# Layer norm scaling moved to VectorE with a lookahead of two pairs, four exp buffers, and an up-projection split in halves

## The chip, the cores and the metric

The kernel runs on one core of a Trainium2 chip. The metric is device time in microseconds (us) of one execution. A core has five engines that run at the same time, each through its own instructions in order: TensorE (PE, matrix products, whose weight loads are listed apart as PEld), VectorE (DVE), ScalarE (ACT), GpSimd (POOL) and SyncE (SP, here only for DMA). An instruction that waits on a semaphore holds back all that stands behind it on its engine.

## The reference

```python
xn  = layernorm(x)                               # x: 2048 tokens x 448, no gain or bias
q, k, v = split(xn @ wqkv)                       # 16 heads of 28
pq, pk  = q @ w_phi[h], k @ w_phi[h]             # 28x28 per head
phi_q = concat(softmax(pq), softmax(-pq))        # 56 features per head
phi_k = concat(softmax(pk), softmax(-pk))
kv, z = phi_k.T @ v, sum(phi_k, over tokens)     # needs every token
o     = (phi_q @ kv) / (phi_q @ z + 1e-6)
h     = xn @ w1 + b1                             # 448 -> 1792
out   = x + o @ wo + mish(h) @ w2
```

## The kernel before, in words

The 2048 tokens are 16 tiles of 128; a pair is two tiles, so there are 8 pairs. Everything stays in SBUF.

**Start.** Loads go out on the queues of SP, ACT and POOL. The 28x28 matrices of `w_phi` are laid as blocks on the diagonal of `Wbd`, which POOL has set to zero; four small DMAs on POOL's queue do it (lines 234 to 236). `w_trans` and `w_mm` fold `Wbd` into the key and query weights once (`Wp`), so that pk and pq come straight from xn.

**Pair loop (lines 472 to 494).** For pair j: `ln` takes statistics on DVE (`bn_stats`, `bn_aggr`), 1/sqrt(var + eps) on POOL (`ln_rstd`, lines 257 and 259), and the scaling `xn = (x - mean) * rstd` (`ln_norm`, line 263) on DVE for pairs 0 and 1 and on POOL for pairs 2 to 7. `xT` transposes xn on PE, and ACT copies it to `xnT`. `vproj` and `kproj` are 8 matmuls each; DVE copies v out of PSUM (line 314), and `kexp` takes exp(pk) and exp(-pk) on ACT into one of two buffers `Ek` (line 330). `knorm` sums each head on DVE (line 335), takes the reciprocal (line 337), and POOL multiplies (line 338), which makes `phi_k`; it runs one pair behind. `qproj` and `qexp` do half of a 512-token group of pq per pair, and give exp(pq), exp(-pq) as `EqT`. `masks` on POOL (lines 240 to 246) stands in pair 2.

**Up-projection loop (lines 499 to 507).** 28 steps n, each with 8 matmuls of the up-projection (`ffn1`, line 420: two halves of 512 tokens, in two PSUM banks) and one Mish on ACT (line 430). After step 5 stands `kvz` (128 matmuls, line 365): kv and z for all heads, masked by DVE into `KVZ`. From step 6 on each step also does `nd` of one tile: 4 matmuls for each sign (line 384) into banks 6 (sign 0) and 7 (sign 1), which hold numerator and denominator, and five DVE operations (lines 390 to 398) and one on POOL that divide them. The two signs are unnormalised exps, so line 391 forms the ratio of the two softmax sums. Three steps later `oTr` transposes the result (line 406).

**Down-projection (lines 433 to 451).** For each tile 14 matmuls with `w2` and 4 with `wo` into one bank; DVE adds x, and SP stores.

**Order.** The program is written out engine by engine in the order of the Python calls. The class `Prog` adds the semaphore waits by itself from the names that each operation reads (`r`), writes (`w`) and the PSUM banks that it uses (`x`). A buffer's name in `w` makes the operation wait for the last readers; a bank in `x` makes it wait for the other engines' last use of that bank.

Of the kernel before, what the change touches and what calls it, by code (L numbers as in the profile page):

```python
# [12 lines left out]
D = 448  # L13
# [144 lines left out]
def _kernel(es, nc, x2, A_wqkv, A_w_phi, A_wo, B_w1, B_b1, B_w2, out2):  # L158
# [38 lines left out]
    hm = [sb(f"hm{i}", [P, FC, 1024]) for i in range(2)]  # L197
    hm0 = hm[0].rearrange("p a b -> p (a b)")
    EK0 = 7 * 1024
    Ek = [hm0[:, EK0 + i * 4 * D:EK0 + (i + 1) * 4 * D].rearrange("p (t s f) -> p t s f", t=2, s=2) for i in range(2)]  # L200
    WT = hm0[0:KP, 0:2 * KC * D].rearrange("p (w c n) -> p w c n", w=2, c=KC)
    phik = hm[1].rearrange("p a b -> p (a b)").rearrange("p (t f) -> p t f", t=NT)
    rq = [sb(f"rq{i}", [P, 2, H], FP32) for i in range(2)]
# [139 lines left out]

    def qproj(tc, gp):
        for u in range(2):
# [67 lines left out]
    def ffn1(n):  # L413
        tcp, fc = n // FC, n % FC
        b = 2 * (n % 2)
        def f(e):
            for u in range(2):
                for c in range(KC):
                    o = tcp * 1024 + u * 512
                    i = e.matmul(PS[:, b + u, :], W1[:, c, fc * P:(fc + 1) * P], xnT[:, c, o:o + 512],  # L420
                                 start=(c == 0), stop=(c == KC - 1))
# [117 lines left out]
```

## Time and profile before

| | |
|---|---|
| three runs | 208.52, 210.96, 212.55 us (median 210.96) |
| the profiled execution | 212.34 us, of which the span of the trace is 210.4 us |
| PE busy | 181.3 us (86% of the span) |
| ACT busy | 84.5 us (40%) |
| DVE busy | 83.3 us (40%) |
| POOL busy | 76.6 us (36%) |
| TensorE clock granted, mean | 0.959 of full speed |

How to read it: the shares are means over stages that differ. The chain of work that ended last is 65% PE, 17% POOL, 9% ACT, 4% DVE and 3% DMA. The span falls into the start and the pair loop (to about 84 us), the up-projection loop (84 to 153 us) and the down-projection (153 us to the end). In rows of matmuls a group's duration reaches from the start of its first to the modelled end of its last; the next group can start before that end.

### The profile page before, as it was taken

How to read it: one execution, taken by the hardware profiler on the slowest of the kernel's cores; microseconds unless marked ns; L12 is line 12 of the kernel's file. 1: busy time of each engine (PE TensorE's matmuls, PEld its weight loads, DVE VectorE, ACT ScalarE, POOL GpSimd, SP SyncE). 2: the span in 40 equal slices, each digit the busy share in tenths (PEclk: the TensorE clock that was granted, in tenths of full speed). 3: DMA queues.
4: the chain of work that ended last, by engine and by line, in shares of the span. 5: the costliest groups of instructions: out<-in, count | busy, mean ns of one | idle time of the engine just before them, and what ended most of it. 6: DMA issues, size and time to landing. Idle time of an engine off the chain costs nothing.

```text
span 210.4 us, 2756 instructions
## 1 busy us (share of the span) xinstructions
PE 181.3 (86%) x1153; PEld 98.0 (47%) x1153; DVE 83.3 (40%) x160; ACT 84.5 (40%) x94; POOL 76.6 (36%) x70
## 2 busy tenths in 40 slices
PE   0587689395894896899999999999999999999994
PEld 0545355142452443349645555554455555555551
DVE  1524085471961564001377777773011212112121
ACT  2536562808438573962246666667720000000000
POOL 8366449999996329200033333442000000000000
PEclk9999699887899797999999999999999999999999
DMA  6999800000000000000000000000001011010101
GB/s 164 281 311 274 241 2 0 0 0 5 2 0 0 0 0 0 3 2 0 3 0 0 3 0 0 3 0 0 3 0 44 29 40 44 22 44 22 47 22 44
DMA packets 7180, 8.69 MB, mean 41 GB/s; under 512 B 576, under 2 KB 6464, under 8 KB 7168
## 3 DMA queue, kind: packets, MB, share of 16 engines
q1 hardware_dynamic: 6544, 8.09, 13.5%
q10 hardware_dynamic: 464, 0.40, 0.6%
q8 instruction: 9, 0.15, 0.3%
q0 software_dynamic: 160, 0.03, 0.1%
q14 instruction: 3, 0.02, 0.0%
HBM read 6.68 MB, written 1.84 MB: 40 GB/s over the span
## 4 chain that ended last, share of the span: by engine, by line
PE 65%; POOL 17%; ACT 9%; DVE 4%; DMA 3%; issue 1%; ACTq 0%; POOLq 0%; DVEq 0%
PE PS L439 20%; PE PS L420 19%; POOL xn L263 7%; POOL hm L338 6%; PE PS L444 6%; PE PS L310 4%; PE PS L384 4%; ACT hm L330 3%; PE PS L365 3%; PE PS L323 3%; DMA Wbd<-in_A_w_phi_dram 3%; ACT EqT L356 2%; PE PS L406 2%; PE PS L349 2%; POOL rstd L259 1%; PE PS L284 1%
## 5 line engine op out<-in xcount | busy, mean ns | idle before, releaser
L420 PE MATMUL PS<-xnT,W 112*128 112x512 bf16 x224 | 52.5, 381 | 0.6 <-ACT hm L430 0.6
L439 PE MATMUL PS<-W,hm 128*128 128x448 bf16 x224 | 45.0, 353 | 0.0
L430 ACT ACTIVATE hm<-PS,b1T 128x1024 bf16<-128x1024 f32 x28 | 31.2, 1114 | 28.2 <-PE PS L420 28.1
L420 PEld LDWEIGHTS PS<-xnT,W 112*128 112x128 bf16 x224 | 21.0, 98 | 23.3 <-ACT hm L430 1.4
L449 DVE TENSOR_TENSOR out_sb<-PS,x_all 128x448 bf16<-128x448 f32 x16 | 10.0, 625 | 54.5 <-PE PS L444 54.5
L439 PEld LDWEIGHTS PS<-W,hm 128*128 128x128 bf16 x224 | 21.9, 98 | 20.6
L338 POOL TENSOR_TENSOR hm<-hm,rSk 128x1792 bf16<-128x1792 bf16 x8 | 25.7, 3217 | 9.3 <-DVE rSk L337 9.2
L310 PE MATMUL PS<-Wqkv,xnT 112*128 112x448 bf16 x64 | 19.0, 457 | 11.1 <-ACT xnT L301 11.1
L330 ACT ACTIVATE hm<-PS 128x896 bf16<-128x896 f32 x16 | 13.8, 914 | 26.3 <-POOL hm L338 17.1
L263 POOL TENSOR_SCALAR xn<-x_all,mv,rstd 128x448 bf16<-128x448 bf16 x12 | 22.3, 1867 | 0.6
L314 DVE CAST v_ext<-PS 128x896 bf16<-128x896 f32 x8 | 8.8, 1094 | 32.7 <-PE PS L310 32.7
L399 POOL TENSOR_TENSOR o_sb<-t_0,rden 128x448 bf16<-128x448 f32 x8 | 7.5, 943 | 31.8 <-DVE rden L398 31.8
L349 PE MATMUL PS<-xnT,Wp 112*112 112x512 bf16 x64 | 16.4, 402 | 2.0 <-ACT EqT L356 2.0
L356 ACT ACTIVATE EqT<-PS 112x1024 bf16<-112x1024 f32 x16 | 15.6, 1037 | 3.3 <-PE PS L349 3.3
L310 PEld LDWEIGHTS PS<-Wqkv,xnT 112*128 112x128 bf16 x64 | 7.0, 119 | 20.7 <-ACT xnT L301 13.5
L323 PE MATMUL PS<-Wp,xnT 112*128 112x448 bf16 x64 | 15.9, 399 | 0.6 <-ACT hm L277 0.6
L335 DVE TENSOR_REDUCE Sk<-hm 128x64 f32<-128x1792 bf16 x8 | 16.0, 1995 | 0.0
L444 PE MATMUL PS<-Wo,EqT 112*128 112x448 bf16 x64 | 14.8, 352 | 0.0
L399 POOL TENSOR_TENSOR o_sb<-t_1,rden 128x448 bf16<-128x448 f32 x8 | 7.5, 943 | 12.5 <-DVE rden L398 12.5
L349 PEld LDWEIGHTS PS<-xnT,Wp 112*112 112x112 bf16 x64 | 8.1, 135 | 7.3 <-ACT EqT L356 2.5
L323 PEld LDWEIGHTS PS<-Wp,xnT 112*128 112x128 bf16 x64 | 6.9, 111 | 8.7 <-issue 3.7
L251 DVE BATCH_NORM_STATS2 stats<-x_all 128x6 f32<-128x448 bf16 x16 | 9.2, 614 | 4.3 <-DMA x_all<-in_A_x_dram 4.3
(51 smaller groups left out, 153.8 us busy)
## 6 DMA issues: line engine op xcount, KB each, us to landing
W<-in_B_w_dram SPq DMA_DIRECT2D x2, 1568.0 KB, 18.8
out_dram<-out_sb SPq DMA_DIRECT2D x16, 112.0 KB, 1.7
x_all<-in_A_x_dram SPq DMA_DIRECT2D x1, 896.0 KB, 10.3
Wqkv<-in_A_wqkv_dram SPq DMA_DIRECT2D x2, 392.0 KB, 7.6
x_all<-in_A_x_dram SPq DMA_DIRECT2D x2, 224.0 KB, 4.4
x_all<-in_A_x_dram SPq DMA_DIRECT2D x1, 448.0 KB, 7.6
Wqkv<-in_A_wqkv_dram ACTq DMA_DIRECT2D x1, 392.0 KB, 5.0
Wo<-in_A_wo_dram SPq DMA_DIRECT2D x1, 392.0 KB, 22.0
```

What stands on the lines that cost most here:

```text
L263: eng(lambda v: v.tensor_scalar(xn[t % NXN][:, :], x_all[:, t, :], mv[:, t, 0:1], rstd[:, t:t + 1], op0=ALU.subtract, op1=ALU.mult), r=[f" ...
L310: i = e.matmul(PS[:, 2 + u, 0:D], xnT[:, c, t * P:(t + 1) * P], Wqkv[:, c, 2 * D:3 * D], start=(c == 0), stop=(c == KC - 1))
L323: i = e.matmul(PS[:, 4 + u, 0:D], xnT[:, c, t * P:(t + 1) * P], Wp[:, 1, c, :], start=(c == 0), stop=(c == KC - 1))
L330: act(lambda a, s=s: a.activation(Ek[j % 2][:, :, s, :], PS[:, 4:6, 0:D], ACT.Exp, scale=(1.0 if s == 0 else -1.0)), w=[f"Ek{j % 2}{s}"], ...
L335: dve(lambda v: v.tensor_reduce(Sk[b][:, :], Ek[b][:, :, :, :].rearrange("p t s (h f) -> p (t s h) f", f=DH), AX.X, ALU.add), r=[f"Ek{b}0" ...
L338: pool(lambda g: g.tensor_tensor(phik[:, 2 * j:2 * j + 2, :].rearrange("p t (k f) -> p (t k) f", f=DH), Ek[b][:, :, :, :].rearrange("p t s ...
L349: i = e.matmul(PS[0:KP, 6 + u, :], Wp[:, 0, c, g * KP:(g + 1) * KP], xnT[:, c, tc * 512:(tc + 1) * 512], start=(c == 0), stop=(c == KC - 1))
L356: act(lambda a, s=s: a.activation(EqT[:, s, 2 * gp:2 * gp + 2, tc * 512:(tc + 1) * 512], PS[0:KP, 6:8, :], ACT.Exp, scale=(1.0 if s == 0 e ...
L420: i = e.matmul(PS[:, b + u, :], W1[:, c, fc * P:(fc + 1) * P], xnT[:, c, o:o + 512], start=(c == 0), stop=(c == KC - 1))
L430: act(lambda a: a.activation(hm[tcp][:, fc, :].rearrange("p (u n) -> p u n", u=2), PS[:, b:b + 2, :], ACT.Mish, bias=b1T[:, fc:fc + 1]), r ...
L439: i = e.matmul(PS[:, b, 0:D], hm[t // 8][:, fc, o:o + P], W2[:, fc, :], start=(fc == 0), stop=False)
L444: i = e.matmul(PS[:, b, 0:D], oT[:, c, t * P:(t + 1) * P], Wo[:, c, :], start=False, stop=(c == KC - 1))
```

## The change

Five things change. The layer norm scaling of pairs 2 to 7 moves from POOL to DVE (`ln_b`), and the statistics and the scaling of a pair are now issued two pairs ahead of its projections. The transposes of pair j+1 stand in front of `vproj(j)` and no longer behind `kexp(j)`. There are four `Ek` buffers, and `knorm` runs two pairs behind. The four `Wbd` DMAs go out on ACT's queue. In the up-projection loop the two halves of `ffn1` are issued apart, with the `nd` matmuls of sign 1 between them and those of sign 0 behind; `kvz` and all `nd` come one step later. (`vevac` is the copy of v, which stood inside `vproj`; `nd_mm` is the matmuls of `nd`, `nd` what is left of it.)

```diff
-    Ek = [hm0[:, EK0 + i * 4 * D:EK0 + (i + 1) * 4 * D].rearrange("p (t s f) -> p t s f", t=2, s=2) for i in range(2)]
+    Ek = [hm0[:, EK0 + i * 4 * D:EK0 + (i + 1) * 4 * D].rearrange("p (t s f) -> p t s f", t=2, s=2) for i in range(4)]
...
-        dma("POOL", Wbd[DH * j:DH * (j + 1), :, DH * j:DH * (j + 1)],
+        dma("ACT", Wbd[DH * j:DH * (j + 1), :, DH * j:DH * (j + 1)],
...
+    def ln_a(j):
+        for t in (2 * j, 2 * j + 1):
+            ln_stats(t)
+        for t in (2 * j, 2 * j + 1):
+            ln_aggr(t)
+        ln_rstd(2 * j, 2)
+
+    def ln_b(j):
+        for t in (2 * j, 2 * j + 1):
+            ln_norm(t, dve)
...
-    ln(0, dve)
+    ln_a(0)
     w_trans(1, 0)
     w_trans(1, 1)
+    ln_b(0)
     xT(0)
+    ln_a(1)
     w_mm(1, 0)
     w_mm(1, 1)
-    ln(1, dve)
-    ln(2, pool)
+    ln_b(1)
     for j in range(NP):
+        if j + 2 < NP:
+            ln_a(j + 2)
+        if j + 1 < NP:
+            xT(j + 1)
         vproj(j)
+        vevac(j)
+        if j + 2 < NP:
+            ln_b(j + 2)
         if j == 0:
             w_trans(0, 0)
             w_trans(0, 1)
         kproj(j)
         kexp(j)
-        if j + 1 < NP:
-            xT(j + 1)
         if j == 0:
             w_mm(0, 0)
             w_mm(0, 1)
         if j >= 1:
             qproj((j - 1) // 2, (j - 1) % 2)
             qexp((j - 1) // 2, (j - 1) % 2)
-        if j + 3 < NP:
-            ln(j + 3, pool)
+        if j >= 2:
+            knorm(j - 2)
         if j == 2:
             masks()
...
-        if j >= 1:
-            knorm(j - 1)
     qproj(3, 1)
     qexp(3, 1)
+    knorm(NP - 2)
     knorm(NP - 1)
-    KV_AT = 5
+    KV_AT = 6
     for n in range(2 * FC):
-        ffn1(n)
+        m = n - KV_AT - 1
+        ffn1_mm(n, 0)
+        if 0 <= m < NT:
+            nd_mm(m, 1)
+        ffn1_mm(n, 1)
+        mish(n)
+        if 0 <= m < NT:
+            nd_mm(m, 0)
+            nd(m)
         if n == KV_AT:
             kvz()
-        m = n - KV_AT - 1
-        if 0 <= m < NT:
-            nd(m)
         if 0 <= m - 3 < NT:
             oTr(m - 3)
```

On POOL, in the pair loop from the first product for `phi_k` (`hm<-hm,rSk`) on; `xn` is the scaling, `rstd` the two operations of `ln_rstd`. Before:

```order
L338 TENSOR_TENSOR hm<-hm,rSk 128x1792
L257 TENSOR_SCALAR rstd<-mv 128x2
L259 TENSOR_TENSOR rstd<-rstd,mhalf 128x2
L263 TENSOR_SCALAR xn<-x_all,mv,rstd 128x448 x2
L240 MEMSET mask 112x116
L242 AFFINE_SELECT mask<-mask 112x116 x2
L245 MEMSET v_ext 128x256
L246 CAST KVZ<-mask 112x32
L338 TENSOR_TENSOR hm<-hm,rSk 128x1792
```

With the change:

```order
L336 TENSOR_TENSOR hm<-hm,rSk 128x1792
L240 MEMSET mask 112x116
L242 AFFINE_SELECT mask<-mask 112x116 x2
L245 MEMSET v_ext 128x256
L246 CAST KVZ<-mask 112x32
L257 TENSOR_SCALAR rstd<-mv 128x2
L259 TENSOR_TENSOR rstd<-rstd,mhalf 128x2
L336 TENSOR_TENSOR hm<-hm,rSk 128x1792
```

The scaling is gone from POOL. The masks now stand between the first product and the `rstd` of pair 5; each later `rstd` still stands behind a product of an earlier pair.

On DVE, one turn of the pair loop (pair 4); `v_ext` is the copy of v, `Sk` and `rSk` belong to `knorm`. Before, and then with the change:

```order
L314 CAST v_ext<-PS 128x32x28
L251 BN_STATS stats<-x_all 128x6 x2
L254 BN_AGGR mv<-stats 128x2 x2
L335 TENSOR_REDUCE Sk<-hm 128x64
L337 RECIPROCAL rSk<-Sk 128x64
```

```order
L251 BN_STATS stats<-x_all 128x6 x2
L254 BN_AGGR mv<-stats 128x2 x2
L467 CAST v_ext<-PS 128x32x28
L263 TENSOR_SCALAR xn<-x_all,mv,rstd 128x448 x2
L333 TENSOR_REDUCE Sk<-hm 128x64
L335 RECIPROCAL rSk<-Sk 128x64
```

The statistics come ahead of the copy of v, and the scaling stands between that copy and the sums.

On PE, the start of the up-projection loop, through the first two steps with `nd` (`PS<-KVZ,EqT`); `PS<-xnT,W` is the up-projection and `PS<-v_ext,hm` is `kvz`. Before, and then with the change:

```order
L420 MATMUL PS<-xnT,W 128x512 x48
L365 MATMUL PS<-v_ext,hm 112x116 x128
L420 MATMUL PS<-xnT,W 128x512 x8
L384 MATMUL PS<-KVZ,EqT 128x120 x8
L420 MATMUL PS<-xnT,W 128x512 x8
```

```order
L418 MATMUL PS<-xnT,W 128x512 x56
L363 MATMUL PS<-v_ext,hm 112x116 x128
L418 MATMUL PS<-xnT,W 128x512 x4
L381 MATMUL PS<-KVZ,EqT 128x120 x4
L418 MATMUL PS<-xnT,W 128x512 x4
L381 MATMUL PS<-KVZ,EqT 128x120 x4
```

One step of the up-projection more stands ahead of `kvz`, and each later step is cut into halves of four matmuls with four of `nd` behind each.

## Rows read from the trace of the kernel before

**Rows 1.** Windows: stretch, its length, busy by engine (instructions), TensorE clock, DMA share, GB/s.

```profile
31.00:66.00 35.00, 24.99 (x129) 12.91 (x129) 18.87 (x27) 17.86 (x21) 34.20 (x24) 0.90 0.00 1
81.00:84.00 3.00, 3.00 (x9) 1.32 (x8) 0.42 (x1) 0.21 (x1) 3.00 (x2) 0.52 0.00 0
```

**Rows 2.** Who waited for whom: us in total, times, longest us.

```profile
ACT hm L330 <- POOL hm L338: 17.1, 4, 5.5
```

**Rows 3.** Chain of waits, 56 to 66 us: start us, us, what.

```profile
56.39 3.72 POOL xn L263 x2
60.11 3.19 POOL hm L338
...
63.33 1.73 ACT hm L330 x2
65.06 0.92 ACT xnT L301
```

**Rows 4.** Timeline of POOL: start us, us, line, operation, shapes [idle before].

```profile
42.06 0.20 POOL L240 MEMSET mask<- 112x116 f32 x1
...
43.98 3.25 POOL L338 TENSOR_TENSOR hm<-hm,rSk 128x1792 bf16<-128x1792 bf16 x1
47.20 0.24 POOL L257 TENSOR_SCALAR rstd<-mv 128x2 f32<-128x2 f32 x1
47.52 0.72 POOL L259 TENSOR_TENSOR rstd<-rstd,mhalf 128x2 f32<-128x2 f32 x1
```

**Rows 5.** Timeline of DVE in the start and the pair loop.

```profile
6.87 0.70 DVE L263 TENSOR_SCALAR xn<-x_all,mv,rstd 128x448 bf16<-128x448 bf16 x2 [1.18 <-POOL rstd L259]
...
32.74 1.09 DVE L314 CAST v_ext<-PS 128x896 bf16<-128x896 f32 x1 [1.07 <-PE PS L310]
...
45.43 1.99 DVE L335 TENSOR_REDUCE Sk<-hm 128x64 f32<-128x1792 bf16 x1
47.45 0.55 DVE L337 RECIPROCAL rSk<-Sk 128x64 f32<-128x64 f32 x1
```

**Rows 6.** Timeline of PE in the start and the pair loop.

```profile
10.26 0.97 PE L284 MATMUL PS<-Wbd,hm 112*112 112x112 bf16 x8 [1.81 <-DMA Wbd<-in_A_w_phi_dram]
...
22.98 0.94 PE L284 MATMUL PS<-Wbd,hm 112*112 112x112 bf16 x8 [2.67 <-ACT Wp L288]
...
59.49 1.68 PE L323 MATMUL PS<-Wp,xnT 112*128 112x448 bf16 x8
61.01 0.61 PE L298 MATMUL PS<-ident,xn 128*112 128x128 bf16 x8
61.46 1.89 PE L349 MATMUL PS<-xnT,Wp 112*112 112x512 bf16 x8
...
76.66 1.89 PE L349 MATMUL PS<-xnT,Wp 112*112 112x512 bf16 x8
80.58 3.18 PE L349 MATMUL PS<-xnT,Wp 112*112 112x512 bf16 x8 [2.03 <-ACT EqT L356]
```

**Rows 7.** Timeline of PE and DVE in one step of the up-projection loop.

```profile
113.50 0.59 PE L384 MATMUL PS<-KVZ,EqT 112*128 112x120 bf16 x8
...
114.16 1.89 PE L420 MATMUL PS<-xnT,W 112*128 112x512 bf16 x8
114.43 0.17 DVE L391 TENSOR_TENSOR rq<-PS,rq 128x16 f32<-128x16 f32 x1
114.64 0.64 DVE L393 TENSOR_TENSOR t_0<-PS,rq 128x464 f32<-128x464 f32 x1
...
116.01 0.59 PE L384 MATMUL PS<-KVZ,EqT 112*128 112x120 bf16 x8
```

**Rows 8.** Timeline of the DMA issues on POOL's and SP's queues.

```profile
1.82 2.63 POOL L169 DMA_DIRECT2D Wbd<-in_A_w_phi_dram  x4
...
5.22 12.51 SPq L169 DMA_DIRECT2D Wo<-in_A_wo_dram  x1
```

**Rows 9.** DMA issues: queue, count, KB each, median us from issue to landing.

```profile
Wqkv<-in_A_wqkv_dram ACTq DMA_DIRECT2D x1, 392.0 KB, 5.0
```

More of the change, by code (lines that the diff above doesn't have):

```diff
@@ L313, in vproj @@
             pe(f, r=[f"xT{j}", "Wv"], x=[2 + u])
-        dve(lambda v: v.tensor_copy(v_ext[:, 2 * j:2 * j + 2, :, 0:DH],
-                                    PS[:, 2:4, 0:D].rearrange("p t (h d) -> p t h d", d=DH)),
-            w=[f"v{j}"], x=[2, 3])
     def kproj(j):
@@ L329, in kexp @@
         for s in range(2):
-            act(lambda a, s=s: a.activation(Ek[j % 2][:, :, s, :], PS[:, 4:6, 0:D], ACT.Exp,
-                                            scale=(1.0 if s == 0 else -1.0)), w=[f"Ek{j % 2}{s}"], x=[4, 5])
+            act(lambda a, s=s: a.activation(Ek[j % 4][:, :, s, :], PS[:, 4:6, 0:D], ACT.Exp,
+                                            scale=(1.0 if s == 0 else -1.0)), w=[f"Ek{j % 4}{s}"], x=[4, 5])
     def knorm(j):
         b = j % 2
-        dve(lambda v: v.tensor_reduce(Sk[b][:, :], Ek[b][:, :, :, :].rearrange("p t s (h f) -> p (t s h) f", f=DH),
-                                      AX.X, ALU.add), r=[f"Ek{b}0", f"Ek{b}1"], w=[f"Sk{b}"])
+        q = j % 4
+        dve(lambda v: v.tensor_reduce(Sk[b][:, :], Ek[q][:, :, :, :].rearrange("p t s (h f) -> p (t s h) f", f=DH),
+                                      AX.X, ALU.add), r=[f"Ek{q}0", f"Ek{q}1"], w=[f"Sk{b}"])
         dve(lambda v: v.reciprocal(rSk[b][:, :], Sk[b][:, :]), r=[f"Sk{b}"], w=[f"rSk{b}"])
@@ L339, in knorm @@
             phik[:, 2 * j:2 * j + 2, :].rearrange("p t (k f) -> p (t k) f", f=DH),
-            Ek[b][:, :, :, :].rearrange("p t s (h f) -> p (t s h) f", f=DH),
+            Ek[q][:, :, :, :].rearrange("p t s (h f) -> p (t s h) f", f=DH),
             ap_on(rSk[b][:, 0:1], [[1, 4 * H], [0, DH]]), ALU.mult),
-            r=[f"Ek{b}0", f"Ek{b}1", f"rSk{b}"], w=[f"phik{j}"])
+            r=[f"Ek{q}0", f"Ek{q}1", f"rSk{b}"], w=[f"phik{j}"])
     def qproj(tc, gp):
@@ L378, in kvz, with nd_mm, f @@
                     r=["mask"], w=["KVZa0"], x=[6])
-    def nd(t):
-        for s in range(2):
-            def f(e, s=s):
+    def nd_mm(t, s):
+            def f(e):
                 for g in range(QG):
@@ L387, in nd @@
             pe(f, r=[f"Eq{t // 4}{gp}{s}" for gp in range(2)] + [f"KVZa{s}", "KVZ1"], x=[6 + s])
+    def nd(t):
         i = t % 2
@@ L411, in oTr, with ffn1_mm @@
             w=[f"oT{t}"], x=[4])
-    def ffn1(n):
+    def ffn1_mm(n, u):
         tcp, fc = n // FC, n % FC
@@ L416, in f, with mish @@
         def f(e):
[L417 to L421, printed above, removed]
-            return i
-        pe(f, r=["W1"] + [f"xT{j}" for j in range(4 * tcp, 4 * tcp + 4)], x=[b, b + 1])
+            for c in range(KC):
+                o = tcp * 1024 + u * 512
+                i = e.matmul(PS[:, b + u, :], W1[:, c, fc * P:(fc + 1) * P], xnT[:, c, o:o + 512],
+                             start=(c == 0), stop=(c == KC - 1))
+            return i
+        pe(f, r=["W1"] + [f"xT{4 * tcp + 2 * u}", f"xT{4 * tcp + 2 * u + 1}"], x=[b + u])
+    def mish(n):
+        tcp, fc = n // FC, n % FC
+        b = 2 * (n % 2)
         if tcp:
@@ L428, in ffn1 @@
         else:
-            rr = ["Ek00", "Ek01", "Ek10", "Ek11"]
+            rr = [f"Ek{i}{u}" for i in range(4) for u in range(2)]
         act(lambda a: a.activation(hm[tcp][:, fc, :].rearrange("p (u n) -> p u n", u=2), PS[:, b:b + 2, :], ACT.Mish,
@@ L462, in ln, with vevac @@
             ln_norm(t, eng)
-    ln(0, dve)
+    def vevac(j):
+        dve(lambda v: v.tensor_copy(v_ext[:, 2 * j:2 * j + 2, :, 0:DH],
+                                    PS[:, 2:4, 0:D].rearrange("p t (h d) -> p t h d", d=DH)),
+            w=[f"v{j}"], x=[2, 3])
+    def ln_a(j):
[8 more added lines that the diff above has]
+    ln_a(0)
     w_trans(1, 0)
     w_trans(1, 1)
+    ln_b(0)
     xT(0)
+    ln_a(1)
     w_mm(1, 0)
     w_mm(1, 1)
-    ln(1, dve)
-    ln(2, pool)
+    ln_b(1)
     for j in range(NP):
+        if j + 2 < NP:
+            ln_a(j + 2)
+        if j + 1 < NP:
+            xT(j + 1)
         vproj(j)
+        vevac(j)
+        if j + 2 < NP:
+            ln_b(j + 2)
         if j == 0:
```

## The prediction, made before the changed kernel was run

> **What bounds the kernel now.** I read the windows first, then the waits, the chain of waits, and the timelines of POOL, DVE and PE. In the pair loop from 31 to 66 us POOL is busy 34.20 of 35.00 us while PE is busy 24.99 [rows 1]: POOL is the bound there. The chain shows how: scaling of pair 7 (3.72 us) to 60.11, the product for phi_k of pair 3 (3.19), then ACT's two exps, which waited for that product because there are only two `Ek` buffers, then the copy to xnT, and PE goes on at 66.0 [rows 3]. ACT waited 17.1 us in all for POOL in this way [rows 2]. POOL's turn is a product (3.22 from its start to the next operation), two rstd operations (1.04) and the scaling (3.72), some 8.0 us [rows 3, 4]. PE's own work for a pair, from start to start at full clock, is 1.52 for `kproj` and as much for `vproj`, 0.45 for `xT` and 1.73 for half a `qproj` (its 1.89 less 0.16, by which a group's modelled end overlaps the next: 59.49 + 1.68 is 0.16 past 61.01): 5.2 us [rows 6].
>
> A second cost hangs on the idle time. After a wait of 2.03 us the last `qproj` takes 3.18 us where the same eight matmuls took 1.89 [rows 6]; the granted clock in 81 to 84 us is 0.52 [rows 1], so mostly the 1.2 GHz level, and after the wait a stretch runs slow that costs about 1.3 us (3.18 - 1.89).
>
> In the up-projection loop a step lasts 2.51 us (113.50 to 116.01) but PE's work in it is `nd` and `oTr` with 0.66 (113.50 to 114.16) and `ffn1` with 1.89 less the same 0.16, 1.73: 2.39 [rows 7]. So PE waits about 0.1 us per step, and the next `nd` starts only when DVE has let go of banks 6 and 7.
>
> **The pair loop after the change.** The scaling costs 0.70 us per pair on DVE [rows 5] in place of 3.72 on POOL [rows 3]. That row was taken with POOL idle. In the new order POOL is idle beside each scaling too: its next product waits for DVE's reciprocal, which stands behind the scaling. The far bound is POOL's 3.72; I take the row of the same instruction on the same engine.
>
> But POOL and DVE now form a ring, since each `rstd` stands on POOL behind the product of an earlier pair, and the sums on DVE behind the scaling that waits for that `rstd`. One turn: reciprocal done, handover about 0.08 (estimate; handovers in these rows are 0.02 to 0.1), product 3.22, rstd 1.04, handover 0.05, scaling 0.70, sums 2.02, reciprocal 0.55 [rows 4, 5]: 7.66 us. That is hardly under 8.0. The gain therefore does not come from the turn itself, but from when the ring starts, from how few turns there are (pairs 5, 6 and 7), and from what no longer follows the last one.
>
> *Start of the ring.* In the trace of before the copy of v of pair 2 ends at 33.83 (32.74 + 1.09) [rows 5]. What PE does ahead of it changes so: `w_mm(0,1)` at 22.98 waited for ACT [rows 6], where the copy of xT(1), 0.92 [rows 3], no longer stands ahead; xT(3), 0.45, now stands in front of `vproj(2)`. That is about 0.5 earlier, and the short wait for the xnT copy in front of `vproj(2)` is gone. I take 0.8 (between 0 and 1.4), so 33.0. Scaling of pair 4, sums and reciprocal of pair 0: 33.0 + 0.70 + 2.57 = 36.3.
>
> *The ring.* The product of pair 0 runs to 39.6, then the masks, 1.92 (42.06 to 43.98 [rows 4]), which now delay the `rstd` of pair 5, to 41.5; rstd to 42.6, scaling of pair 5 from 42.6. Two turns of 7.66 later, at 57.9, comes the scaling of pair 7, done at 58.6: 1.5 earlier than 60.11.
>
> New waits that this makes: `xT(j+1)` now stands ahead of `vproj(j)` on PE, so a late scaling also holds back `vproj(j)`, `kproj(j)`, and on DVE the copy of v, which stands in front of the next scaling. For pair 5: xT from 43.3, even at the slow clock 0.9, then `vproj(4)` at most 3.2, copy of v to 48.5. The scaling of pair 6 waits for its rstd until 50.2 anyway, so 1.7 us of slack cover it.
>
> *Behind the ring.* PE goes on at 58.65 with xT(7), vproj(6), kproj(6), qproj, vproj(7), kproj(7), and starts the next `qproj` 0.45 + 4 x 1.52 + 1.73 = 8.3 us later at full clock; PE has waited over 2 us by then, so I add one slow stretch of 1.3: 68.3. No exp waits for a buffer: the product of pair 2 ends near 56.8, before `kproj(6)` is done. From that `qproj` to the last one it took 3.92 us (76.66 to 80.58) [rows 6], set by kexp(7) and qexp on ACT, and nothing in that changes. So the last `qproj` starts at 72.2 instead of 80.58: **8.4 us** gained. On POOL the products of pairs 5 to 7 (3 x 3.2) follow the copy of v of pair 7 and the sums of pair 5, near 70.5, and end near 80.5; `kvz` needs them, and seven steps of the up-projection (7 x 1.73) cover that until 87.5. With the old place of `kvz`, one step earlier, 5 us would still be left, so moving it costs and gains nothing.
>
> **The Wbd DMAs.** `w_mm(1,0)` waited 1.81 us for Wbd until 10.26 [rows 6]. On POOL's queue the four issues took 2.63 us [rows 8]. The nearest row on ACT's queue is Wqkv, 5.0 us from issue to landing [rows 9]. Issued behind the memset of Wbd from about 1.5 at POOL's pace, the last lands near 9.1; bounds 8.45 (no wait) and 10.26 (no gain). ACT's issues end near 4.2, and its first copy waits for Wqkv's landing anyway. Whatever is gained here, xT(1), which now stands ahead of `vproj(0)`, takes up (0.9 at the slow clock): I count it in the 0.8 above. The Trainium skill, "DMA: Bandwidth & Descriptors", section "Queues, rings and completion order", says that all DMAs of ACT share one ring on each DMA engine, consumed in order. By that rule Wbd queues behind Wqkv and lands perhaps at 10.3 (estimate), and the total is about 0.5 us worse; no row here shows two DMAs on ACT's queue.
>
> **The up-projection loop.** After the change bank 7 is free after line 393, not after line 396, and bank 6 has half a step more. The new ring: `nd` of sign 1 (0.21), half of `ffn1` (0.87), `nd` of sign 0 (0.21 and 0.16 until its end), lines 391 and 393 (0.21 and 0.64) and about 0.1 of handovers: 2.40 [rows 7], against 2.39 of PE's work. So 2.51 becomes 2.40, 15 intervals: **1.6 us** gained; at best 1.8, at least nothing if a split group starts later. The masked copy `KVZ` (DVE) is now covered by only half a `ffn1`; one time 0.1 at most.
>
> **Sum.** 8.4 + 1.6 = 10.0 us. The profiled execution took 212.34 us (span 210.4), so the same execution would take 202.3 (span 200.4). It lies 1.4 above the median of the runs, 210.96, so I predict **201.0 us**.
>
> **Rivals.**
> - *PE keeps its clock.* If the waits in front of xT(7) and the last `qproj` (about 2.4 and 2.0 us) do not lower it, 2 x 1.3 us fall away: 198.4. For it: the waits are short. Against: one of 2.03 did lower it [rows 6].
> - *The split halves do not pipeline.* Two more changes of group per step; if each shows the 0.16 us by which a group's end overlaps the next [rows 6], the step becomes 2.39 + 0.32 = 2.71 and the loop loses 16 x 0.20 = 3.2 instead of gaining 1.6: 205.8; half of it gives 203.2. Against: the change from `nd` to `oTr` to `ffn1` shows no gap.
> - *The ring is longer.* If the slow clock, or a scaling that takes longer beside other work, uses up the 1.7 us of slack, each microsecond counts twice: 204 to 207.
> - *Slower than before: ACT's queue blocks.* SP's issue of Wo was held for 12.51 us, to 17.7, behind the large loads [rows 8]. If ACT's issues for Wbd were held so long and Wbd landed 5.0 later [rows 9], at 22.7, `w_mm(1,0)` with all of PE behind it would start 12.4 us later than at 10.26 [rows 6]: 213.4, slower than before. It decides from a landing at 20.3 on, 10.0 later than now. Against: ACT's queue has only Wqkv ahead, and SP's hold came at its tenth DMA.
>
> **How the numbers follow.** Forecast 0.65, clock kept 0.13, halves do not pipeline 0.12, longer ring 0.05, ACT blocked 0.05. The forecast's own range is 197.5 to 204.5: start of the ring 0.6 either way, loop 1.6 down to nothing, and 2 us of scatter between runs (208.52 to 212.55). With the clock case below and half of the split case above, the range is 196.0 to 205.5. A measurement of this kernel can tell about 2%, 4.2 us, from no change: faster means below 206.7, slower above 215.2. Nearly all of the first three cases and half of the longer ring lie below 206.7; I take 0.90, 0.07 and 0.03.
>
> **What would show it.** Right: no wait of ACT's exps on POOL; scaling rows on DVE of 0.35 each; scalings of pairs 5, 6 and 7 about 7.7 us apart, each waiting for rstd; the last `qproj` near 72 us; steps of 2.40 us. Wrong: a wait of `w_mm` on Wbd beyond 10.3; steps of 2.5 us or more; scalings of pairs 6 and 7 that wait for the copy of v instead.

## The result, and the profile after

| | before | after |
|---|---|---|
| median of the runs compared | 210.73 us (208.52 to 212.55, 4 runs) | 201.22 us (200.9 to 202.23, 4 runs) |
| profiled execution, span | 212.34, 210.4 us | 200.96, 199.0 us |
| start of the last `qproj` | 80.58 us | 69.27 us |
| interval of an up-projection step | 2.51 us | 2.47 us |
| TensorE clock granted, mean of the span | 0.959 | 0.983 |

The ratio of the two is 0.959, with a 95% interval of 0.9505 to 0.9676: faster. The medians are 9.5 us apart, where 10.0 were forecast. Executions that were slow for their kernel are left out of the ratios (here the one of 212.55), so that a ratio is not the quotient of the medians beside it; this one stands for 8.6 us. The page of the changed kernel, span and busy times by engine:

```profile
span 199.0 us, 2766 instructions
...
PE 176.7 (89%) x1153; PEld 97.9 (49%) x1153; DVE 84.4 (42%) x172; ACT 85.4 (43%) x94; POOL 51.7 (26%) x54
```

POOL lost 24.9 us of work (76.6 to 51.7), most of it the six pairs of scalings at 3.72 [rows 3]; DVE, which took them over at 0.70 a pair, is busy only 1.1 us longer (83.3 to 84.4). That has not made the kernel faster by 24.9 us; the waits say why (engine, line, the releaser, us in all, times, longest us):

```profile
ACT hm L327 <- PE PS L320: 12.0, 8, 3.3
...
DVE xn L263 <- POOL rstd L259: 10.5, 5, 4.0
...
PE PS L298 <- DVE xn L263: 4.8, 3, 2.3
```

ACT's exps (now line 327) wait only for their matmuls, and no more for POOL's product [rows 2]. In its place DVE waits for POOL's `rstd`, and PE for DVE's scaling: the ring that the prediction described. It can be followed on two engines. DVE, scalings of pairs 4 to 7 and one reciprocal (start us, us, line, operation, what ended the idle time before it):

```profile
31.98 0.69 DVE L263 TENSOR_SCALAR xn<-x_all,mv,rstd 128x448 bf16<-128x448 bf16 x2
...
34.64 0.55 DVE L335 RECIPROCAL rSk<-Sk 128x64 f32<-128x64 f32 x1
...
41.50 0.70 DVE L263 TENSOR_SCALAR xn<-x_all,mv,rstd 128x448 bf16<-128x448 bf16 x2 [3.98 <-POOL rstd L259]
...
49.02 0.70 DVE L263 TENSOR_SCALAR xn<-x_all,mv,rstd 128x448 bf16<-128x448 bf16 x2 [2.10 <-POOL rstd L259]
...
56.54 0.70 DVE L263 TENSOR_SCALAR xn<-x_all,mv,rstd 128x448 bf16<-128x448 bf16 x2 [2.10 <-POOL rstd L259]
```

and POOL in the first turn, with the masks in it:

```profile
35.27 3.21 POOL L336 TENSOR_TENSOR hm<-hm,rSk 128x1792 bf16<-128x1792 bf16 x1 [5.43 <-DVE b1T L516]
38.43 0.19 POOL L240 MEMSET mask<- 112x116 f32 x1
...
40.33 0.33 POOL L257 TENSOR_SCALAR rstd<-mv 128x2 f32<-128x2 f32 x1
...
44.80 3.21 POOL L336 TENSOR_TENSOR hm<-hm,rSk 128x1792 bf16<-128x1792 bf16 x1 [3.33 <-DVE rSk L335]
```

The reciprocal of pair 0 ends at 35.19, the product follows, the masks fill 38.43 to 40.3, only then comes `rstd`, and the scaling of pair 5 starts at 41.50. From there on a turn is 7.52 us (41.50, 49.02, 56.54), and the product at 44.80 waits 3.33 us for DVE's reciprocal: the operations of the ring run one after the other on the two engines. Beside POOL's product DVE has, in these turns, only statistics and the copy of v.

PE of the changed kernel, at the places that matter:

```profile
10.23 0.97 PE L284 MATMUL PS<-Wbd,hm 112*112 112x112 bf16 x8 [1.95 <-DMA Wbd<-in_A_w_phi_dram]
...
23.15 0.62 PE L284 MATMUL PS<-Wbd,hm 112*112 112x112 bf16 x8 [2.21 <-ACT Wp L288]
...
41.95 1.01 PE L298 MATMUL PS<-ident,xn 128*112 128x128 bf16 x8 [2.33 <-DVE xn L263]
...
56.99 0.74 PE L298 MATMUL PS<-ident,xn 128*112 128x128 bf16 x8 [2.02 <-DVE xn L263]
...
69.27 3.57 PE L347 MATMUL PS<-xnT,Wp 112*112 112x512 bf16 x8 [2.03 <-ACT EqT L354]
```

The first row answers to that at 10.26 of before [rows 6]: the Wbd DMAs gave nothing. The last answers to 80.58. Beside it the windows (start and end, length, busy time and instructions of PE, PEld, DVE, ACT, POOL, granted clock, DMA share, GB/s):

```profile
41.90:45.00 3.10, 3.04 (x14) 1.72 (x15) 3.06 (x5) 1.02 (x1) 0.20 (x1) 0.53 0.02 5
57.00:60.00 3.00, 3.00 (x21) 1.82 (x22) 2.96 (x4) 1.02 (x1) 0.16 (x1) 1.00 0.00 0
...
69.20:72.70 3.50, 3.44 (x9) 1.67 (x10) 3.31 (x4) 0.01 (x1) 3.50 (x2) 0.53 0.00 0
```

After the waits of 2.33 and 2.03 us PE ran mostly at the 1.2 GHz level (0.53); after the one of 2.02 in front of xT(7) it kept 2.4 GHz (1.00).

Last, one step of the up-projection loop, PE and DVE:

```profile
108.27 0.38 PE L381 MATMUL PS<-KVZ,EqT 112*128 112x120 bf16 x4
...
108.49 1.03 PE L418 MATMUL PS<-xnT,W 112*128 112x512 bf16 x4
...
109.35 0.37 PE L381 MATMUL PS<-KVZ,EqT 112*128 112x120 bf16 x4
...
109.83 0.17 DVE L390 TENSOR_TENSOR rq<-PS,rq 128x16 f32<-128x16 f32 x1 [0.55 <-PE PS L381]
110.04 0.64 DVE L392 TENSOR_TENSOR t_0<-PS,rq 128x464 f32<-128x464 f32 x1
...
110.73 0.22 PEld L381 LDWEIGHTS PS<-KVZ,EqT 112*128 112x128 bf16 x4 [0.42 <-DVE t_0 L392]
110.74 0.38 PE L381 MATMUL PS<-KVZ,EqT 112*128 112x120 bf16 x4
```

`nd` of sign 1 at 110.74 still waits for line 392, 0.42 us of PE's weight loads; DVE's line 390, for its part, starts when sign 0 is done. The ring that was forecast is there, but it is 2.47 us long (108.27 to 110.74).

### The profile page after: what moved, and what is told of

It reads as the page before. It is cut to its first block, busy times and chain, and to the rows that moved or that the text cites. A ratio compares the mean times of both kernels' runs of the same rounds, so it can differ in the third digit from the quotient of the medians.

```text
span 199.0 us, 2766 instructions
## 1 busy us (share of the span) xinstructions
PE 176.7 (89%) x1153; PEld 97.9 (49%) x1153; DVE 84.4 (42%) x172; ACT 85.4 (43%) x94; POOL 51.7 (26%) x54
## 4 chain that ended last, share of the span: by engine, by line
PE 72%; POOL 7%; DVE 7%; ACT 6%; DMA 4%; issue 1%; ACTq 0%; DVEq 0%; POOLq 0%
PE PS L418 21%; PE PS L441 21%; PE PS L446 6%; POOL hm L336 5%; PE PS L310 5%; PE PS L381 4%; DMA Wbd<-in_A_w_phi_dram 4%; PE PS L347 4%; PE PS L363 3%; PE PS L320 3%; DVE Sk L333 3%; ACT EqT L354 2%; PE PS L405 2%; ACT hm L327 2%; PE PS L284 1%; PE PS L298 1%
## 5 line engine op out<-in xcount | busy, mean ns | idle before, releaser
L418 PE MATMUL PS<-xnT,W 112*128 112x512 bf16 x224 | 54.7, 379 | 0.9 <-ACT hm L432 0.9
L418 PEld LDWEIGHTS PS<-xnT,W 112*128 112x128 bf16 x224 | 20.3, 98 | 19.5 <-ACT hm L432 1.4
L310 PE MATMUL PS<-Wqkv,xnT 112*128 112x448 bf16 x64 | 16.3, 407 | 0.0
L320 PE MATMUL PS<-Wp,xnT 112*128 112x448 bf16 x64 | 13.5, 353 | 0.4 <-ACT hm L277 0.4
L381 PEld LDWEIGHTS PS<-KVZ,EqT 112*128 112x128 bf16 x128 | 8.3, 98 | 11.0 <-DVE t_0 L392 3.8
L347 PEld LDWEIGHTS PS<-xnT,Wp 112*112 112x112 bf16 x64 | 8.7, 138 | 8.4 <-ACT EqT L354 2.5
L381 PE MATMUL PS<-KVZ,EqT 112*128 112x120 bf16 x128 | 12.1, 217 | 0.5 <-DVE t_1 L392 0.2
L298 PE MATMUL PS<-ident,xn 128*112 128x128 bf16 x64 | 6.5, 257 | 4.8 <-DVE xn L263 4.8
```

The costliest lines, as they stand in the source:

```text
L320: i = e.matmul(PS[:, 4 + u, 0:D], xnT[:, c, t * P:(t + 1) * P], Wp[:, 1, c, :], start=(c == 0), stop=(c == KC - 1))
L347: i = e.matmul(PS[0:KP, 6 + u, :], Wp[:, 0, c, g * KP:(g + 1) * KP], xnT[:, c, tc * 512:(tc + 1) * 512], start=(c == 0), stop=(c == KC - 1))
```

## The experiments

Each time is a median of device us, and each ratio is against the kernel before, run on the same chip. The edits are on the changed kernel, except the one that is on the kernel before.

### Scaling back on POOL (c5_xn_pool)

```diff
-            ln_norm(t, dve)
+            ln_norm(t, dve if j < 2 else pool)
```

> The changed kernel with the scaling of pairs 2 to 7 back on POOL, lookahead, four Ek buffers and split kept. Theory (turns of POOL and DVE pace the loop): POOL's turn is a product, rstd and scaling, 8.0 us, three turns from the first product near 34 to 35; the scaling of pair 7 ends near 60 to 61 instead of 57.2, 204 us. Rival (the place of the scaling does not matter, the buffers and the lookahead do): 201.2. Rival (the scaling on DVE is nearly all of the gain): 208 or more.

205.29 us (204.48 to 207.12; before 211.05), ratio 0.9752 [0.9695, 0.981]. POOL's scalings of pairs 5 and 7:

```profile
42.05 3.71 POOL L263 TENSOR_SCALAR xn<-x_all,mv,rstd 128x448 bf16<-128x448 bf16 x2
...
58.04 3.71 POOL L263 TENSOR_SCALAR xn<-x_all,mv,rstd 128x448 bf16<-128x448 bf16 x2
```

They are two turns of 8.0 us apart, POOL's own turn of before [rows 4], and the last `qproj` starts at 73.77, 4.5 later. So the move itself is worth about 4 us: each turn is hardly shorter, as predicted, but the last scaling ends at 57.2 and not 61.8. Of these 4.5, 3.0 are the length of that last scaling (3.71 against 0.70), 0.95 the two turns, and 0.55 a later start (42.05 against 41.50). All else in the change, without the move, still gives 5.8 us.

### Two exp buffers (c4_two_ek)

```diff
-    Ek = [... for i in range(4)]
+    Ek = [... for i in range(2)]
...
-        if j >= 2:
-            knorm(j - 2)
+        if j >= 1:
+            knorm(j - 1)
...
-    knorm(NP - 2)
```

(`Ek[j % 4]` becomes `Ek[j % 2]` throughout.)

> The changed kernel with two Ek buffers and knorm one pair behind again. Theory (a ring of POOL and DVE paces the loop, and the two pairs of distance give it one turn less and keep ACT's exps from waiting): four turns of 7.5 us instead of three, ACT waits for POOL's products again at some pairs, last qproj 2 to 4 us later than 69.3, 204 us. Rival (the scaling that left POOL is all of it): 201.2. Rival (the buffers are nearly all of it): 208 or more.

205.21 us (203.38 to 206.87), ratio 0.9713 [0.9611, 0.9815]. The wait of before is back:

```profile
ACT hm L327 <- POOL hm L336: 14.7, 5, 4.3
```

The turn is unchanged, 7.52 us (scalings at 44.88, 52.40, 59.92), but pair 4's scaling, at 35.34 in place of 31.98, now waits for a `rstd` behind a product too: four turns in place of three. The last `qproj` starts at 74.03. The extra buffers, with `knorm` two pairs behind, do not speed the ring up; they take a turn out of it.

### Masks out of the ring (c6_masks_early)

```diff
-        if j == 2:
+        if j == 0:
             masks()
+        if j == 2:
```

> The changed kernel with POOL's masks issued in pair 0, where POOL is idle, and no longer between the first product and the rstd of pair 5. Theory (the masks stand in the ring): scalings of pairs 5, 6 and 7 each 1.9 us earlier, last qproj near 67.4, 199.3 us. Rival (PE or DVE has the slack to hide them): 201.2.

200.62 us (200.51 to 200.93), ratio 0.9521 [0.9485, 0.9558]. DVE's scalings of pairs 4 and 5:

```profile
33.60 0.70 DVE L263 TENSOR_SCALAR xn<-x_all,mv,rstd 128x448 bf16<-128x448 bf16 x2
41.12 0.70 DVE L263 TENSOR_SCALAR xn<-x_all,mv,rstd 128x448 bf16<-128x448 bf16 x2 [1.98 <-POOL rstd L259]
```

They are 7.52 apart, where the changed kernel has 9.52 (31.98 to 41.50): the masks were worth 2.0 us in the ring. But the median fell by 0.6 only. In this profile pair 4 is scaled 1.6 later than in the changed kernel (33.60 against 31.98); there the front had run a slow stretch less. The masks in pair 0 are not needed for that stretch: `vproj(1)`, 1.68 us in the profile of the changed kernel and 2.75 here, took 2.80, 3.16 and 2.94 in c1_no_split, c3_wbd_pool and c8_nd_late, where the masks stand as in the changed kernel. The last `qproj` starts at 68.87 here and at 69.94, 70.65 and 70.32 in those three. The step in the ring is confirmed, the size in the total missed; executions at the same mean clock differ by 0.35 (0.983) and by about 1.0 (0.974), and why the rest of the 2.0 does not arrive there is not shown.

### Statistics three pairs ahead (c7_rstd_early)

```diff
     ln_b(1)
+    ln_a(2)
     for j in range(NP):
-        if j + 2 < NP:
-            ln_a(j + 2)
+        if j + 3 < NP:
+            ln_a(j + 3)
```

> The changed kernel with the statistics and rstd three pairs ahead instead of two (the scaling stays two ahead), so that no scaling waits for an rstd behind a product. Theory (the ring of product, rstd, scaling and sums, 7.5 us a turn, paces pairs 5 to 7): the turns fall to DVE's work of some 5.5 us or PE's 5.2, last qproj 5 to 6 us earlier than 69.3, 195.5 us. Rival (DVE is full, or PE's clock sets the pace): under 2 us gained, 199.5 or more.

196.71 us (194.44 to 197.09), ratio 0.9311 [0.9252, 0.937]; the last `qproj` starts at 64.93, 4.3 earlier. With `rstd` ready ahead of time the ring is open. DVE no longer waits for it, but something else shows; the first of the two scalings of pair 7, and what POOL did beside it:

```profile
50.04 2.56 DVE L263 TENSOR_SCALAR xn<-x_all,mv,rstd 128x448 bf16<-128x448 bf16 x1
```

```profile
49.26 3.21 POOL L336 TENSOR_TENSOR hm<-hm,rSk 128x1792 bf16<-128x1792 bf16 x1 [2.02 <-DVE rSk L335]
```

One scaling, 0.39 us elsewhere (0.70 for the two of a pair, which overlap a little), took 2.56, until 52.60; POOL's product ended at 52.47. DVE was held until the product was done. The pairs' scalings took 1.71, 1.62 and 2.87 in place of 0.70.

### The same, scaling between the sums and the reciprocal (c12_scale_late)

Built on c7_rstd_early, for pairs 4 to 7:

```diff
         dve(lambda v: v.tensor_reduce(Sk[b][:, :], ...), ...)
+        if mid is not None:
+            mid()                       # ln_b(j + 2), moved here
         dve(lambda v: v.reciprocal(rSk[b][:, :], Sk[b][:, :]), ...)
```

> The kernel c7 (statistics and rstd three pairs ahead) with one more edit: from pair 2 of the loop on, the scaling stands on DVE between the sums and the reciprocal of knorm, by which time POOL's product of the turn before has ended. Theory (in c7 the scalings of pairs 5, 6 and 7 took 1.71, 1.62 and 2.87 us instead of 0.70 because each ended only when POOL's product, which ran beside them, had ended): the three rows fall back to 0.70, DVE's turn from some 6.25 to 5.5, 1 to 2 us less than c7's 196.7, about 195.2. Rival (the scalings are slow for another reason, such as TensorE's or ACT's traffic at that time): rows stay above 1.5 us and the time at 196.7.

194.99 us (194.42 to 195.61), ratio 0.9236 [0.9165, 0.9306]. The scaling of pair 7 (that of pair 6, at 46.61, took as long):

```profile
52.27 0.69 DVE L263 TENSOR_SCALAR xn<-x_all,mv,rstd 128x448 bf16<-128x448 bf16 x2
```

POOL waits for the reciprocal behind them, so it is idle, and these scalings are back at 0.69; pair 5's, beside the masks, took 1.40. That the hold came from POOL's work is shown. That the gain of 1.7 us at the median comes from it is not: the last scaling ends at 52.96 here and at 52.91 there, because it now stands behind 2 us of sums, and the last `qproj` starts at 64.99 and 64.93. In the profiles the difference is that this `qproj` ran in 1.93 us here and in 3.37 there.

### The split undone (c1_no_split)

```diff
-    KV_AT = 6
+    KV_AT = 5
...
         ffn1_mm(n, 0)
-        if 0 <= m < NT:
-            nd_mm(m, 1)
         ffn1_mm(n, 1)
         mish(n)
+        if n == KV_AT:
+            kvz()
         if 0 <= m < NT:
             nd_mm(m, 0)
+            nd_mm(m, 1)
             nd(m)
-        if n == KV_AT:
-            kvz()
```

> The changed kernel with the up-projection loop of before: both halves of the up-projection first, then both signs of nd, kvz one step earlier. Theory (the gain is in the pair loop; the split gave only 15 x 0.04, since a step went from 2.51 to 2.47): last qproj still near 69.3, steps back at 2.51, 201.8 us. Rival (the split gave the 1.6 that was forecast): 202.8 us. Rival (the split costs more than it gives): 200 us or less.

202.1 us (200.8 to 202.68), ratio 0.9586 [0.9508, 0.9664]. Two steps:

```profile
105.56 0.59 PE L381 MATMUL PS<-KVZ,EqT 112*128 112x120 bf16 x8
...
108.06 0.59 PE L381 MATMUL PS<-KVZ,EqT 112*128 112x120 bf16 x8
```

2.50 us per step, against 2.47 with the split: some 0.5 us in all, and the total agrees with that within its scatter.

### The split alone (c2_split_only, on the kernel before)

```diff
-        ffn1(n)
-        if n == KV_AT:
-            kvz()
         m = n - KV_AT - 1
+        ffn1_mm(n, 0)
+        if 0 <= m < NT:
+            nd_mm(m, 1)
+        ffn1_mm(n, 1)
+        mish(n)
         if 0 <= m < NT:
+            nd_mm(m, 0)
             nd(m)
+        if n == KV_AT:
+            kvz()
```

> The kernel before with only the split of the up-projection loop and kvz one step later. Theory: pair loop as before, last qproj near 80.6, steps 2.47, 0.6 us faster than before, about 210.2. Rival (the split gives 1.6): 209.1. Rival (the halves cost time in group changes): 211 or more.

210.26 us (207.62 to 212.07, 10 runs), ratio 1.0005 [0.9947, 1.0064]: no difference that can be measured. At a mean clock of 0.983 one execution spans 205.9 us, where two of before span 206.1 and 206.4. Steps of 2.47 here too:

```profile
112.65 0.38 PE L383 MATMUL PS<-KVZ,EqT 112*128 112x120 bf16 x4
...
115.12 0.38 PE L383 MATMUL PS<-KVZ,EqT 112*128 112x120 bf16 x4
```

The last `qproj` was expected near 80.6, as in the profile of before, and starts at 77.73; the part on the clock below uses this.

### The split with the matmuls later (c8_nd_late)

```diff
         ffn1_mm(n, 0)
-        if 0 <= m < NT:
-            nd_mm(m, 1)
         ffn1_mm(n, 1)
         mish(n)
         if 0 <= m < NT:
+            nd_mm(m, 1)
+        if 0 <= m - 3 < NT:
+            oTr(m - 3)
+        if 0 <= m < NT:
             nd_mm(m, 0)
             nd(m)
```

> The changed kernel with the nd matmuls of sign 1 behind both halves of the up-projection, then oTr, then those of sign 0. Theory (a step is 2.47 because the matmuls of sign 1 wait for DVE's line 392 of the tile before, over half an up-projection): the wait goes, steps 2.39, 1.2 us less, 200.0 us. Rival (the step is bound by PE's own work and the group changes): steps stay 2.47, 201.2.

199.45 us (198.93 to 200.32), ratio 0.9467 [0.9425, 0.9509], 1.8 below the changed kernel. The edit also moves `oTr` between the two signs. Steps:

```profile
99.73 1.89 PE L418 MATMUL PS<-xnT,W 112*128 112x512 bf16 x8
...
102.10 1.89 PE L418 MATMUL PS<-xnT,W 112*128 112x512 bf16 x8
```

2.37 us: PE's own work (2.39 by prediction), without a wait. The 1.6 us that the split was to bring are there (15 x 0.10 = 1.5 against the changed kernel), when both halves of the up-projection stand in front of `nd` of sign 1 and give DVE the time. How much of it `oTr` between the signs gives was not tried apart.

### Wbd back on POOL's queue (c3_wbd_pool)

```diff
-        dma("ACT", Wbd[DH * j:DH * (j + 1), :, DH * j:DH * (j + 1)],
+        dma("POOL", Wbd[DH * j:DH * (j + 1), :, DH * j:DH * (j + 1)],
```

> The changed kernel with the four Wbd DMAs back on POOL's queue. Theory (Wbd lands at the same time on either queue, since the first w_mm started at 10.26 before and 10.23 after): w_mm at 10.2, 201.2 us, no difference. Rival (ACT's queue is part of the gain): w_mm later by 1 or more and 202 us or more.

201.59 us (200.97 to 201.99), ratio 0.9568 [0.95, 0.9635]: no difference. PE in the front:

```profile
10.25 0.96 PE L284 MATMUL PS<-Wbd,hm 112*112 112x112 bf16 x8 [1.83 <-DMA Wbd<-in_A_w_phi_dram]
...
22.84 0.62 PE L284 MATMUL PS<-Wbd,hm 112*112 112x112 bf16 x8 [2.21 <-ACT Wp L288]
...
23.75 3.16 PE L310 MATMUL PS<-Wqkv,xnT 112*128 112x448 bf16 x8
```

The queue does not matter. The last row shows how the scatter arises: the same wait of 2.21 us as in the changed kernel, but `vproj(1)` behind it takes 3.16 here and 1.68 there (24.06 in the changed kernel).

### All that helped (c9_all)

c6_masks_early, c7_rstd_early and c8_nd_late together (their three diffs).

> c7 (rstd three pairs ahead) with c6 (masks in pair 0) and c8 (nd of sign 1 behind both halves). Theory (the three act on different waits): c7's 196.7 less 1.6 for the steps and 0.3 for the masks, which no longer stand in a ring: 194.8. Rival (they overlap): 196 or more.

193.19 us (191.31 to 194.5), ratio 0.9079 [0.8993, 0.9164]: the lowest median of all, 8.0 below the changed kernel. Its executions took 191.95 and 191.31 us at a mean clock of 0.999 and 0.998, and 194.50 and 194.44 at 0.982 and 0.981. PE at the end of the pair loop, in the first of these:

```profile
64.17 1.93 PE L347 MATMUL PS<-xnT,Wp 112*112 112x512 bf16 x8 [2.03 <-ACT EqT L354]
...
70.55 8.81 PE L418 MATMUL PS<-xnT,W 112*128 112x512 bf16 x40 [0.99 <-ACT hm L432]
```

### The last wait filled (c10_ffn_first)

On c9_all, the first up-projection step is issued ahead of the last `qproj`:

```diff
+    ffn1_mm(0, 0)
+    ffn1_mm(0, 1)
     qproj(3, 1)
```

> c9 with the first step of the up-projection moved ahead of the last qproj on PE, into the wait of 2.0 us for ACT's exps. Theory (that wait and the slow stretch behind it, 3.4 us for eight matmuls instead of 1.9, are both on the path): 2 us less than c9, 192.8. Rival (the first Mish, behind the last exps and a table load of 1.28 on ACT, sets the start of step 2 either way): under 0.7 less.

193.77 us (193.2 to 194.29), ratio 0.9179 [0.9121, 0.9238]: no gain.

```profile
63.90 1.93 PE L347 MATMUL PS<-xnT,Wp 112*112 112x512 bf16 x8 [0.30 <-ACT EqT L354]
...
70.28 10.36 PE L418 MATMUL PS<-xnT,W 112*128 112x512 bf16 x40 [2.72 <-ACT hm L432]
```

The wait moved: 0.30 in place of 2.03, then 2.72 in place of 0.99. The next steps need a bank that Mish frees, and ACT's first Mish still follows the last exps. The same 40 matmuls then took 10.36 us in place of 8.81; from 70.2 to 73.0 the granted clock was 0.50. So the median of c9_all is lower by executions that lost nothing to the clock: at 0.981 to 0.982 c9_all spans 192.4 and 192.5 us, this kernel 191.4, 192.2 and 192.4.

### The last wait filled, scaling late (c11_best)

c10_ffn_first with the place of the scaling from c12_scale_late.

> c10 with c12's place of the scaling. Theory: as much less than c10 as c12 is less than c7, 1 to 1.5 us: 191.5. Rival (PE's own work of 5.2 us a pair hides it): no difference from c10.

195.18 us (194.57 to 195.69), ratio 0.9246 [0.9188, 0.9303]: a miss. The scalings took 0.69 to 0.70 each time, 5.67 apart, but pair 7's ends at 52.71, later than in c10_ffn_first (51.88), on which it is built; 0.73 of that is a later start of the first `w_mm` (10.73 against 10.00). Behind the wait of 2.72 the same 40 matmuls took longer still:

```profile
71.12 11.92 PE L420 MATMUL PS<-xnT,W 112*128 112x512 bf16 x40 [2.72 <-ACT hm L434]
```

## Why the prediction came out as it did

*The bound.* POOL's turn of 8.0 us bounded the pair loop, and ACT's wait for it was the coupling: c5_xn_pool and c4_two_ek, each of which puts one of the two back, lose about 4 us each. The lookahead and the new place of `xT` were not taken back by themselves, so what each of them gives is not shown. That the turn itself would gain little (7.66 against 8.0) was right; it measured 7.52: from the product's start to the scaling 4.22 (44.80 to 49.02; forecast 3.22 + 1.04 + 0.05 = 4.31), and from there to the next product 3.30 (forecast 0.70 + 2.57 + 0.08 = 3.35).

*Start of the ring.* Forecast 36.3, measured 35.19: 1.1 early, because `vproj(1)` ran in 1.68 us in this profile, at full clock, and in 3.05 in that of before. Where it ran slow, the forecast was right: c8_nd_late, with the same pair loop and 2.94 us for `vproj(1)`, scaled pair 4 at 33.03 (forecast 33.0) and pairs 5 to 7 at 42.57, 50.08 and 57.60 (forecast 42.6, 50.3 and 57.9). The delay by the masks was forecast to 42.6 and came to 41.50, the same 1.1. c6_masks_early shows that the masks cost 2.0 there.

*Behind the ring.* The forecast added a slow stretch of 1.3 in front of xT(7). PE did wait there, 2.02 us, and did not slow down, and neither did it in c1_no_split, c3_wbd_pool, c6_masks_early and c8_nd_late. So the last `qproj` came at 69.27 and not 72.2: 2.9 early, of which 1.1 + 2 x 0.14 are the ring and 1.3 the stretch; the rest, 0.25, comes from xT(7), which started 0.45 after the scaling did, behind the first of the pair's two, where the forecast had 0.75, behind both. The two steps behind the ring measured 8.36 (56.99 to 65.35) and 3.92, against 8.3 and 3.92. The slow stretch behind the last `qproj` did come (3.57). The rival in which PE keeps its clock came true at one of its two places.

*The clock.* Here the account of the sum falls short: except for the stretch in front of xT(7) it took the slow stretches of the two kernels as equal. The profile of before (mean clock 0.959) has five stretches at about half clock (0.52 to 0.57 granted), near 25, 42, 52, 69 and 82 us; that of the changed kernel (0.983) has two, near 43 and 70. Two of the five lengthened the way to the last `qproj`, as matmuls that take 1.68 us at full clock; before:

```profile
23.72 3.05 PE L310 MATMUL PS<-Wqkv,xnT 112*128 112x448 bf16 x8
...
67.64 3.19 PE L323 MATMUL PS<-Wp,xnT 112*128 112x448 bf16 x8
```

c2_split_only has the pair loop of before, and a profile with only two stretches (0.983), near 40 and 50 us:

```profile
23.91 1.68 PE L310 MATMUL PS<-Wqkv,xnT 112*128 112x448 bf16 x8
...
66.31 1.68 PE L323 MATMUL PS<-Wp,xnT 112*128 112x448 bf16 x8
...
77.73 1.93 PE L349 MATMUL PS<-xnT,Wp 112*112 112x512 bf16 x8 [2.03 <-ACT EqT L356]
```

Its two, and those of before near 42 and 52, fall where POOL sets the pace and is busy almost without a gap (34.20 of 35.00 us [rows 1]); the first stretch of the changed kernel falls into the slack that the prediction counted (pair 6 still waits 2.10 for `rstd`). So with no stretch on the path of either, the last `qproj` moves from 77.73 to 69.27, by 8.46: the 8.4 of the sum was right. The other 2.85 of the 11.3 between the two profiles are the two stretches above.

The same mean clock does not mean the same cost. At 0.983 two executions of before spanned 206.1 and 206.4, and two of the changed kernel 199.0 and 198.9: 7.3 us, that is 8.46 and some 0.5 of the loop, less 1.64 by which the last `qproj` of the changed kernel ran slow (3.57 against 1.93). At 0.974 to 0.975 six of before spanned 207.6 to 208.7 and two of the changed kernel 199.5 and 200.3: about 8.2. That the medians came within 0.5 us of the forecast is in part luck: the loop gave 1.1 less than forecast, and the executions of before that were compared lost some 0.5 more to the clock. Against the 8.6 of the ratio the forecast is 1.4 too high.

*The up-projection loop.* Forecast 2.40 and 1.6 us, measured 2.47 and 0.5. The mechanism was right, the term for handovers mis-sized. The measured ring, from 108.27: `nd` of sign 1 0.22, half of `ffn1` 0.86, `nd` of sign 0 to its modelled end 0.37, line 390 0.21 and line 392 0.64; these make 2.30, as in the sum of the prediction. What is left, 0.17, is handovers: 0.11 from PE to line 390 (109.72 to 109.83), 0.06 from line 392 through the weight load to the next group (110.68 to 110.74). I had put 0.1 for both; 15 x 0.07 is the missing 1.1 us. c8_nd_late confirms this from the other side: with half a step of time given to DVE, the step falls to 2.37. Both ends of my bound (1.8, nothing) held.

*The Wbd DMAs.* I took a landing at 9.1 by POOL's pace, and counted the gain in the 0.8; the last of them landed at 10.10, 7.28 us after its issue began, by the chain of waits of the changed kernel (start us, us, what):

```profile
2.82 7.28 DMA Wbd<-in_A_w_phi_dram
```

The bound "no gain" was the right value, as c3_wbd_pool shows. The Trainium skill, "DMA: Bandwidth & Descriptors", section "Queues, rings and completion order", has the rings of one queue consumed in order. The order in this trace agrees: PE had Wqkv, issued first on that queue, at 5.69, and Wbd landed 4.4 us later. The estimate of 10.3 by that rule was nearer than mine, but the prediction gives no working for it, and the order in ACT's ring is not shown to be the cause, since from POOL's queue the landing was the same (10.12 in c3_wbd_pool, 10.13 before). What sets it is open.

*The rivals.* The halves pipeline: the weight load and the group behind `nd` of sign 1 follow without a gap (110.74, 110.96). The ring did not grow, though a slow stretch fell into it. ACT's queue did not block, and the landing at 10.10 is far from the 20.3 from which on that rival makes the kernel slower (SP's hold came at its ninth DMA, not its tenth as the prediction says). ACT's timeline in the front:

```profile
1.43 2.01 ACTq L169 DMA_DIRECT2D Wbd<-in_A_w_phi_dram  x4
3.48 1.28 ACT L277 ACT_TABLE_LOAD   x1 [3.48 <-issue]
6.72 1.73 ACT L277 ACTIVATE hm<-PS 112x896 bf16<-112x896 bf16 x2 [1.96 <-PE PS L274]
```

The four issues took 2.01 us, less than on POOL [rows 8], the table load came behind them, and the first copy still waited for PE.

*The scaling rows.* 0.70 per pair was right (0.39 for each of the two, not 0.35, since they overlap), and for the reason given (POOL idle beside it). c7_rstd_early shows the price where it fails: up to 2.87. The Trainium skill, "SBUF — State Buffer", section "Who interferes with whom", says that VectorE in its two-port modes and GpSimd share a pair of ports and that the later one blocks for the whole instruction of the other; the rows 50.04 and 49.26 agree with that.

## What to carry to other kernels

When work moves from a busy engine to an idle one, look for the ring that the two then form, and cut it where it costs least: here the tiny `rstd` behind the product kept DVE and POOL in turns, and issuing it a pair earlier gave 4.5 us more, about as much as moving the scaling itself. A split group gives the other engine time only if the work in front of the waiting half is long enough; measure it from the release, not from the group's start. Before a gain is put down to an edit, count the slow stretches of the clock in both traces and see which of them lie on the path, because one more or one less looks like a gain; the mean granted clock also counts those that stand where PE would have waited anyway.

## What the hardware showed that was not expected

- A wait of PE of 2.0 to 2.7 us lowers the clock in some places and not in others. Slow behind it: 2.67 and 2.03 (before [rows 6]), 2.33 and 2.03 (changed kernel), 2.21 (c3_wbd_pool), 2.72 (c10_ffn_first, c11_best). Full speed: 2.21 and 2.02 (changed kernel), 2.67 and 2.03 (c2_split_only), 2.03 (c9_all, c12_scale_late). The waits of 2.03, 2.21 and 2.67 stand on both sides, each at the same place of the program. What decides is open.
- A scaling on DVE beside a product on POOL was held until the product's end (2.56 us for 0.39).
- The last of four DMAs of 6.1 KB landed at the same time, 10.10 to 10.13 us, from ACT's queue as from POOL's, though its issue began at 2.82 on the one and at 3.87 on the other.
- From 10 to 20 us the granted clock reads 1.00 in both profiles, yet `vproj(0)` took 3.19 us in both, where a later one takes 1.68. Either the reading misses a slow start, or these matmuls were slow for another reason; no run here decides.
